# Forty-three offsets to the ranks of a list scheduler, in a fused cosine-attention and highway kernel

## The chip, the cores and the metric

The kernel runs on one core of a Trainium2 chip. The metric is the device time of one execution in microseconds (us). A core has TensorE (PE: matmuls; PEld is its weight load), VectorE (DVE), ScalarE (ACT), GpSimd (POOL) and SyncE (SP, which here only issues DMAs). Each engine executes its own instructions in the order in which the program lists them, and waits on semaphores for what others produce.

## The reference

Eight batches of twelve heads, 448 positions of 64 elements; the result goes as 3584 tokens of 768 into a highway layer.

```python
def _attn_ref(q, k, v, tau):                       # q, k, v: (8, 12, 448, 64)
    q_n = q / (np.linalg.norm(q, axis=-1, keepdims=True) + 1e-06)
    k_n = k / (np.linalg.norm(k, axis=-1, keepdims=True) + 1e-06)
    scores = np.matmul(q_n, k_n.transpose(0, 1, 3, 2)) / tau
    attn = softmax(scores)                          # rows
    return np.matmul(attn, v)

def _moe_ref(x, w_h, w_t, b_t):                     # x: (3584, 768), w: (768, 768)
    H = np.maximum(x @ w_h, 0.0)
    T = 1.0 / (1.0 + np.exp(-(x @ w_t + b_t)))
    return T * H + (1.0 - T) * x

x = _attn_ref(q, k, v, tau).transpose(0, 2, 1, 3).reshape(3584, 768)
out = _moe_ref(x, w_h, w_t, b_t)
```

## The kernel before

**The attention part** goes through 24 *quads* of four heads of one batch (three quads to a batch). A quad's steps, with the line at which the profile shows them:

- *load*: `load_qk` loads q and k as f32 (L312, issued by SP), `load_v` loads v (L334). Six buffers hold raw q and k, two hold v.
- *squares* (L395 on ScalarE, L397 on VectorE, L399 and L411 on GpSimd: two halves), for some quads *folds* on GpSimd that add halves of the squares (L459, L465), and sums of each head on VectorE (L432).
- *inverse root*: for the first quads on ScalarE by a logarithm and an exponential (L488, L497); later, for a batch at a time, on VectorE, by a shift (L521), a subtraction from a constant (L527) and two Newton steps of three operations (L547, L549, L551).
- *norms* (L588, GpSimd or VectorE): raw times inverse root, in f16 as `qn`; then `qn` is transposed to `qT`, on TensorE (L616) with a copy (L622 and 623), or by a DMA that SP issues (L636).
- *scores*: `quad` has seven column groups; for each TensorE multiplies into the tile `sp` (L692, 4 products, or 8 for a pair of groups), and ScalarE takes the exponential of it with 1/tau into `e` (L703). No maximum is subtracted, since cosines are bounded.
- *probabilities times V* in two rounds: `av` (L743), six groups of 14 products, then two groups, into one PSUM tile `u` (a single buffer). The column of V beyond the 64 holds a constant, so that the row sum comes out too. VectorE takes the reciprocal (L776) and scales into the f16 tile `x` (L794; L786 for the tail rows of two batches).
- *cast of v* to f16 as `vm` (L655, VectorE or ScalarE).

**The feed-forward part** takes the 28 tiles of 128 tokens as soon as their x is complete. x is transposed to `xT` (L842 on TensorE, or L851 as a DMA from SP). Then `quarters` runs four passes: halves 0 and 1 of 384 columns, w_t first and w_h second in each half. A pass is two groups of three matmuls (L886, 128x128 by 128x384), in one PSUM tile. It lands in `pt` or, for w_t in the last six tiles, in `sp`; both names have two buffers. The bias is added by a matmul with a row of ones or on VectorE (L904). ScalarE takes the tanh of the w_t pass (L914). The weights are loaded by GpSimd's queue in four halves (L356; the third and fourth are w_h).

The sigmoid is written by tanh; its factor of two is in the V column. For most tiles VectorE ends a half with `fd` (L972: relu of H minus x), `fh` (L957: times 1+tanh) and `fr` (L979: plus 2x). Some tiles have a gate instead: GpSimd computes (tanh−1)·x in two steps (L925, L929) or VectorE in one (L918), and VectorE ends with `fh` (L957) and `fo` (L964: relu, minus the gate). SP stores the result (L1003, L1009).

**What sets the order.** All steps are recorded as operations of a `Plan` with an engine, an estimated duration, a due time (`pri`) and the operations they need; an operation's number is the order in which it was recorded. Buffers enter as needs (`buf`): the n-th user of a ring of tiles needs all users of the tile that it overwrites. `run` first works out due times backwards from the users of each operation. Then it is a list scheduler: it keeps a clock for each engine in its own model of the chip, and takes the ready operation with the smallest key, in which the due time enters with a weight:

```python
k = (max(s, t + self.NEAR) + (e != "SP") * self.LATE * 1000 * o.pri
     + (e == "PE" and o.kind != mode) * self.MODE, o.pri, o.n)
```

Operations marked "lock" are VectorE operations that the model does not let run beside a GpSimd operation. The order found is the order in which the instructions are emitted. Nothing of the model is in the program: on the chip only the order on each engine and the semaphores count. Between the due times and the scheduler stand these lines, which with an empty `NUDGE` do nothing:

```python
for n, shift in self.NUDGE.items():
    self.ops[n].pri += shift
```

Of the kernel before, what the change touches and what calls it, by code (L numbers as in the profile page):

```python
# [20 lines left out]
class Plan:  # L21
# [9 lines left out]
    LATE = 0.04  # L31
    MODE = 60
    QUEUE = 3000
    NUDGE = {}

    def __init__(self):
        self.ops = []
# [20 lines left out]
    def run(self):  # L58
# [31 lines left out]

        for n, shift in self.NUDGE.items():
            self.ops[n].pri += shift
# [1003 lines left out]
```

## Time and profile before

| | before |
|---|---|
| median of 9 runs | 267.87 us (266.84 to 272.14) |
| the profiled execution | 267.87 us |
| its span, first to last instruction | 266.10 us |
| around the span | 1.77 us |
| mean granted TensorE clock | 0.976 |
| DMA | 58.39 MB, mean 219 GB/s |
| scores L692 | 672 products, 53.5 us |
| exponentials L703 | 168 of 128x896, 926 ns each, 145.6 us |
| probabilities times V L743 | 2688 products, 53.9 us |
| feed-forward matmuls L886 into pt and sp | 672, 114.3 and 13.7 us |

A row of a timeline gives the start and the length in us, the engine, the line, the operation, the output from the input, its shape and how many stand in the row; in brackets the idle time of that engine before it and what was seen to end it. Matmuls overlap: the row of three feed-forward matmuls has 0.65 us, but three rows in a line follow each other at 0.49.

### The profile page before, as it was taken

How to read it: one execution, taken by the hardware profiler on the slowest of the kernel's cores; microseconds unless marked ns; L12 is line 12 of the kernel's file. 1: busy time of each engine (PE TensorE's matmuls, PEld its weight loads, DVE VectorE, ACT ScalarE, POOL GpSimd, SP SyncE). 2: the span in 40 equal slices, each digit the busy share in tenths (PEclk: the TensorE clock that was granted, in tenths of full speed). 3: DMA queues.
4: the chain of work that ended last, by engine and by line, in shares of the span. 5: the costliest groups of instructions: out<-in, count | busy, mean ns of one | idle time of the engine just before them, and what ended most of it. 6: DMA issues, size and time to landing. Idle time of an engine off the chain costs nothing.

```text
span 266.1 us, 9994 instructions
## 1 busy us (share of the span) xinstructions
PE 238.6 (90%) x4252; PEld 137.0 (51%) x4252; DVE 223.1 (84%) x493; ACT 213.3 (80%) x295; POOL 148.7 (56%) x164
## 2 busy tenths in 40 slices
PE   7378666989889999999999999999999999997991
PEld 2135453655546655555555555455555655564650
DVE  3988866899999899898998899989998476479983
ACT  4699999699998999999788978989897888820220
POOL 1289586945584975799649941898163004550000
PEclk9858999999999999999999999999999999999998
DMA  6999999988998999999999999999997951216413
GB/s 204 343 381 367 266 266 247 267 257 263 284 330 271 226 245 268 275 169 199 272 342 167 287 251 212 277 195 200 152 262 118 148 130 39 79 42 156 142 60 118
DMA packets 69853, 58.39 MB, mean 219 GB/s; under 512 B 46128, under 2 KB 66096, under 8 KB 69808
## 3 DMA queue, kind: packets, MB, share of 16 engines
q1 hardware_dynamic: 68208, 55.39, 81.5%
q0 software_dynamic: 1600, 2.36, 4.9%
q8 instruction: 33, 0.54, 0.9%
q14 instruction: 12, 0.10, 0.1%
HBM read 38.14 MB, written 11.01 MB: 185 GB/s over the span
## 4 chain that ended last, share of the span: by engine, by line
PE 56%; DVE 18%; ACT 10%; DMA 10%; issue 3%; SPq 1%; POOL 1%; DVEq 0%; ACTq 0%; POOLq 0%
PE pt L886 28%; PE u L743 13%; PE sp L692 11%; ACT e L703 7%; DMA w<-in_moe_w_h_dram 6%; DVE pt L957 3%; DMA raw<-in_q_dram 3%; DVE pt L972 3%; DVE o L979 3%; PE sp L886 2%; DVE x L794 2%; DVE n L432 2%; PE xp L842 2%; ACT sq L395 1%; DMA xT<-x 1%
## 5 line engine op out<-in xcount | busy, mean ns | idle before, releaser
L703 ACT ACTIVATE e<-sp 128x896 f16<-128x896 f32 x168 | 145.6, 926 | 11.2 <-PE sp L692 10.7
L886 PE MATMUL pt<-w,xT 128*128 128x384 f16 x600 | 114.3, 327 | 4.7 <-DMA w<-in_moe_w_h_dram 2.1
L588 POOL TENSOR_TENSOR qn<-raw,rs 128x448 f16<-128x448 f32 x76 | 74.5, 1012 | 38.3 <-DVE rs L551 19.4
L886 PEld LDWEIGHTS <-xT 128*128 128x128 f16 x672 | 60.2, 98 | 54.9 <-issue 17.9
L692 PE MATMUL sp<-qT,qT 64*64 64x448 f16 x672 | 53.5, 373 | 9.0 <-ACT e L703 7.6
L743 PEld LDWEIGHTS <-e 64*128 64x128 f16 x2688 | 46.4, 95 | 19.1 <-issue 13.3
L743 PE MATMUL u<-vm,e 64*128 64x65 f16 x2688 | 53.9, 192 | 0.0
L957 DVE SCALAR_TENSOR_TENSOR pt<-tt,pt 128x384 f32<-128x384 f16 x56 | 31.4, 561 | 6.8 <-PE pt L886 2.5
L459 POOL TENSOR_TENSOR fold<-sq 128x448 f32<-128x448 f16 x24 | 24.7, 1039 | 14.6 <-ACT sq L395 13.2
L432 DVE TENSOR_REDUCE n<-sq 128x7 f32<-128x448 f16 x48 | 27.7, 608 | 4.9 <-ACT sq L405 3.3
L692 PEld LDWEIGHTS <-qT 64*64 64x64 f16 x672 | 15.1, 105 | 32.1 <-issue 27.8
L972 DVE SCALAR_TENSOR_TENSOR pt<-pt,x 128x384 f32<-128x384 f32 x40 | 22.5, 563 | 8.5 <-PE pt L886 7.1
L914 ACT ACTIVATE tt<-pt 128x384 f16<-128x384 f32 x44 | 22.0, 499 | 8.9 <-PE pt L886 4.0
L395 ACT ACTIVATE sq<-raw 128x896 f16<-128x896 f32 x29 | 27.8, 966 | 0.2 <-DMA raw<-in_q_dram 0.2
L794 DVE TENSOR_TENSOR x<-u,rd 128x384 f16<-128x384 f32 x48 | 24.6, 551 | 0.6
L979 DVE SCALAR_TENSOR_TENSOR o<-x,pt 128x384 f32<-128x384 f16 x40 | 22.1, 552 | 1.0
L914 ACT ACTIVATE tt<-sp 128x384 f16<-128x384 f32 x12 | 5.9, 491 | 20.7 <-DVE sp L904 18.9
L399 POOL TENSOR_TENSOR sq<-raw 128x448 f16<-128x448 f32 x14 | 13.1, 937 | 10.2 <-DMA raw<-in_k_dram 10.2
L886 PE MATMUL sp<-w,xT 128*128 128x384 f16 x72 | 13.7, 326 | 1.7 <-DMA xT<-x 1.7
L776 DVE RECIPROCAL rd<-u 128x12 f32<-128x12 f32 (+1 forms) x48 | 9.7, 201 | 5.4 <-PE u L743 5.0
L411 POOL TENSOR_TENSOR sq<-raw 128x448 f16<-128x448 f32 x14 | 13.2, 940 | 0.0
L655 DVE CAST vm<-vr 128x448 f16<-128x448 f32 (+1 forms) x21 | 12.6, 621 | 0.1
(59 smaller groups left out, 188.4 us busy)
## 6 DMA issues: line engine op xcount, KB each, us to landing
vr<-in_v_dram SPq DMA_DIRECT2D x24, 448.0 KB, 7.1
raw<-in_q_dram SPq DMA_DIRECT2D x23, 448.0 KB, 5.5
raw<-in_k_dram SPq DMA_DIRECT2D x23, 448.0 KB, 6.1
out_dram<-o SPq DMA_DIRECT2D x24, 384.0 KB, 4.1
out_dram<-o SPq DMA_DIRECT2D x8, 192.0 KB, 2.7
w<-in_moe_w_t_dram POOLq DMA_DIRECT2D x2, 576.0 KB, 12.1
w<-in_moe_w_h_dram POOLq DMA_DIRECT2D x2, 576.0 KB, 15.7
qT<-qn SPq DMA_TRANSPOSE x34, 3.8
```

The costliest lines, as they stand in the source:

```text
L395: nc.scalar.activation(o, i, AF.Square)
L432: nc.vector.reduce_sum(n2[:, qd, NT * t + g0 : NT * t + g0 + n], src()[:, g0 : g0 + n, 0:width], axis=AX.X,)
L588: (nc.vector if eng == "DVE" else nc.gpsimd).tensor_mul(st["qn", Q, t][:, :, :].rearrange("p c (h d) -> p h c d", h=2)[:, h0:h1, c0:c1, :] ...
L692: nc.tensor.matmul(sp[64 * half : 64 * half + 64, h, 0:S].rearrange("x (c p) -> x c p", c=C), lhsT=kT[hp, ci, 64 * half : 64 * half + 64], ...
L703: nc.scalar.activation(e[:, o : o + 2 * S].rearrange("x (a p c) -> x a p c", a=2, c=C), st["sp", Q, ci][:, :, 0:S].rearrange("x a (c p) -> ...
L743: nc.tensor.matmul(u[:, s, slot * (D + 1) : (slot + 1) * (D + 1)], lhsT=e[sp, o : o + 128], rhs=vm[sp, 2 * qd + h, c, 0 : D + 1], start=(c ...
L794: nc.vector.tensor_mul(st["x", b][:, :, 4 * qd : 4 * qd + 4, :].rearrange("p t (h s) d -> p t h s d", s=2)[:, :, :, s, :], u[:, s, :, 0:D] ...
L886: nc.tensor.matmul(loc["pt", qi], lhsT=loc["xT"][:, cc, :] if cc < CC else ones_row[:, :], rhs=w_f[w_i][:, cc, ms] if cc < CC else bth[:, ms],
L914: nc.scalar.activation(loc["tt", mh][:, :], loc["pt", qi], AF.Tanh)
L957: nc.vector.scalar_tensor_tensor(out=h, in0=loc["tt", mh][:, :], scalar=1.0, in1=h, op0=ALU.add, op1=ALU.mult)
L972: nc.vector.scalar_tensor_tensor(out=h, in0=h, scalar=0.0, in1=xf()[:, ms], op0=ALU.max, op1=ALU.subtract)
L979: nc.vector.scalar_tensor_tensor(out=loc["o"][:, ms], in0=xf()[:, ms], scalar=2.0, in1=loc["pt", qi], op0=ALU.mult, op1=ALU.add,)
```

## The change

`NUDGE` gets 43 entries: number of an operation, and the shift of its due time in us (negative: earlier). Nothing else is changed; the instructions are the same ones. Since the due time enters the key with weight 0.04, a shift of 10 us is worth 0.4 us of start time in the model, and one early choice can move later ones.

```diff
-    NUDGE = {}
+    NUDGE = {
+        63: -57.5, 121: -57.5, 147: -1, 172: 5, 264: -57.5, 314: 12, 407: 3.5, 427: 12.5, 441:
+        -2.5, 445: 3.5, 454: 1.5, 455: -46, 459: -1, 491: 8, 527: 4, 532: 3.5, 693: 65.5, 707:
+        4, 736: -16.5, 747: 4, 790: 4, 828: 15.5, 871: 10, 976: 8.5, 1001: 3, 1024: -10.5, 1055:
+        2.5, 1068: -7, 1240: 29.5, 1316: 0.5, 1340: 2, 1346: 16, 1366: -8.5, 1369: -24, 1426:
+        37, 1466: -2.5, 1467: -16.5, 1468: -4.5, 1560: 8.5, 1568: 15, 1576: 2, 1581: 15, 1588:
+        58,
+    }
```

By engine, the smallest number of operations whose moving turns the one order into the other: TensorE 29 of 571 (a group of matmuls is one operation), VectorE 63 of 488, ScalarE 16 of 295, GpSimd 12 of 159, SP 12 of 157. TensorE's order differs around 24 to 41 us of the profile of before, 58 to 63, 200, 208 and 227 to 242; from 63 to 198 us its operations stand in the same order. ScalarE's differs around 27 to 64 and 144 to 151.

The moves of which the prediction speaks, with the place in time that the operation had in the profile of before:

| operations | what they are | how they move |
|---|---|---|
| 121 | VectorE, sum of squares of quad 3, half of k | ahead of other steps, near 24 us |
| 445, 172, 491 | ScalarE: a cast of v, squares of quad 8, an exponential of quad 4 | behind their neighbours, 46 to 64 us |
| 790 and neighbours | VectorE, a feed-forward end step near 97 us | behind a reciprocal (operation 671) |
| 693, 976, 1024 | GpSimd, norms of quads 8, 13 and 14 | among GpSimd's other steps |
| 264, 265, 266 | VectorE, inverse root of the fifth batch (L521, L527, L547) | 265 and 266 behind three end steps and a cast, 129 to 134 us |
| 276 | VectorE, squares (L397, 142.78 us) | ahead of the L972 at 139.04 us |
| 314 | GpSimd, squares (L411, 178.95 us) | behind the gate step L925 (183.54), ahead of its L929 (184.53) |
| 1466–1468, 1472, 1473 | TensorE, probabilities times V of quad 22 | some groups earlier among the feed-forward matmuls, from 227 us |
| 1560, 1568, 1576, 1581 | TensorE, groups of three feed-forward matmuls | 1568 and 1581 behind the probabilities times V of the last quad (237.64) |
| 1569, 1570 | VectorE, `fh` L957 (236.34) and `fo` L964 (239.22) | behind the scaling of the last quad (L794, 239.95) |

## Prediction

> **What bounds the kernel now.** The page came first: the busy shares and the chain that ended last.
>
> ```profile
> PE 238.6 (90%) x4252; PEld 137.0 (51%) x4252; DVE 223.1 (84%) x493; ACT 213.3 (80%) x295; POOL 148.7 (56%) x164
> PE 56%; DVE 18%; ACT 10%; DMA 10%; issue 3%; SPq 1%; POOL 1%; DVEq 0%; ACTq 0%; POOLq 0%
> ```
>
> TensorE is 90% busy and holds over half of the chain. The change adds and removes no instruction, so it can only shorten or lengthen waits, and where TensorE loses time decides. The table of windows of 10 us says where (columns: PE, PEld, DVE, ACT, POOL busy, clock, DMA share, GB/s):
>
> ```profile
> 30.00:40.00 10.00, 6.04 (x170) 4.43 (x167) 7.32 (x14) 10.00 (x15) 9.16 (x10) 1.00 1.11 264
> 40.00:50.00 10.00, 7.58 (x162) 4.55 (x158) 6.88 (x14) 8.21 (x13) 7.73 (x9) 1.00 0.98 234
> 130.00:140.00 10.00, 9.22 (x184) 5.00 (x185) 9.56 (x24) 7.84 (x11) 4.18 (x5) 1.00 1.04 286
> 180.00:190.00 10.00, 9.52 (x175) 5.27 (x176) 9.76 (x24) 8.93 (x12) 5.29 (x6) 1.00 0.85 190
> 240.00:250.00 10.00, 8.35 (x77) 5.00 (x76) 9.39 (x20) 1.47 (x3) 0.00 (x0) 1.00 0.62 156
> ```
>
> Before 80 us TensorE is short of work while ScalarE is full (10.00 in 30–40). From 80 to 240 us TensorE is busy at 9.2 to 10.0, and a delay of it is carried on, since no slack is left to absorb it; a saving likewise. From 240 us VectorE (9.39) is the fuller engine: it runs eight steps of 0.56 us at a pitch of 0.47 to 0.66 for each tile of the feed-forward stage, while TensorE needs 4 × 0.98 = 3.9 us.
>
> Next the timelines around each place where the order differs.
>
> ```profile
> 46.44 0.65 PE L886 MATMUL pt<-w,xT 128*128 128x384 f16 x3 [2.05 <-DMA w<-in_moe_w_h_dram]
> 132.73 1.14 PE L886 MATMUL pt<-w,xT 128*128 128x384 f16 x6 [0.34 <-DVE o L979]
> 189.94 0.65 PE L886 MATMUL pt<-w,xT 128*128 128x384 f16 x3 [0.42 <-DVE o L979]
> 243.90 1.15 PE L886 MATMUL sp<-w,xT 128*128 128x384 f16 x6 [1.66 <-DMA xT<-x]
> ```
>
> These four stalls of TensorE, 4.5 us together, are what a new order could reach.
>
> **Part 1, up to 64 us (thirteen shifts): nothing, −0.3 to +0.3.** At 46.44 the queue of TensorE stands until the last half of w_h has landed, and the chain shows 14.79 us of that transfer. Its issue (L356, GpSimd, 31.61 us) waits behind two normalisations on GpSimd. In the new order the sum of squares that they depend on is taken earlier, and the issue would come at about 29.8. But the weight queue q0 carries 2.36 MB from 25 to 46 us without a gap, sharing the engines with the loads of q1: it is never dry, so an earlier issue of the last piece lands at the same time. The changed steps of TensorE, ScalarE and VectorE ahead of the barrier are the same set in both orders and all reach it, since TensorE has 2.05 and ScalarE (next row, 47.46) 0.89 us to spare. On SP a load of q for quad 9 passes a transposition (issue 45.49); the transpositions have 5 us or more from landing to first use. Behind the barrier three ScalarE steps swap places (exponentials, one squaring, one cast); counted through, ScalarE comes to the same step at 64.3 instead of 64.2.
>
> **Part 2, 64 to 128 us: +0.1 (0 to +0.2).** Near 97 us a reciprocal of 0.2 us moves ahead of L957 and its L979, whose reader on TensorE had 0.07 us to spare: 0.2 − 0.07 ≈ 0.1. Other moves (GpSimd's norms for quads 13 and 14, L979 and L957 at 113) have covers of 1 us and more.
>
> **Part 3, 128 to 146 us: −0.5 (−0.9 to +0.4).** Now the first steps of an inverse root stand in the middle of VectorE's evictions:
>
> ```profile
> 129.59 1.08 DVE L527 TENSOR_SCALAR rs<-rs 128x84 int32<-128x84 int32 x1
> 187.65 0.20 DVE L527 TENSOR_SCALAR rs<-rs 128x84 int32<-128x84 int32 x1
> 129.57 1.03 POOL L459 TENSOR_TENSOR fold<-sq 128x448 f32<-128x448 f16 x1
> 136.43 8.22 POOL L588 TENSOR_TENSOR qn<-raw,rs 128x448 f16<-128x448 f32 x8 [5.82 <-DVE rs L551]
> 142.78 1.07 DVE L397 TENSOR_TENSOR sq<-raw 128x896 f16<-128x896 f32 x1
> ```
>
> The same step takes 1.08 us beside a GpSimd fold that ends with it, and 0.20 alone: 0.88 is waiting for GpSimd. The change puts L521 and L527 behind three evictions and a cast, so these come up to 1.3 us sooner and the 0.34 stall at 132.73, plus 0.1 to 0.2 of its after-effect, goes: −0.5. Against it, the squaring L397 (now 142.78) moves ahead of the L972 at 139.04, that is, into GpSimd's run of eight norms of 1.03 each. If it waits as L527 did, it costs up to 0.9 there, and the stall saved comes back: +0.4. I take −0.5, because L397 at 142.78 also lies in that run (136.43 to 144.65) and took 1.07, hardly more than its work. The Trainium skill ("SBUF — State Buffer", Terms) says that the two engines share a port pair that is held for a whole instruction and blocks the other fully. By that rule alone the moved L397 could wait for a whole norm, and this part would be +0.4 instead of −0.5; it speaks against this move.
>
> **Part 4, 176 to 192 us: +0.5 (+0.2 to +1.1).** On GpSimd the second half of a squaring (L411) moves from ahead of one gate to between two gate steps:
>
> ```profile
> 178.95 0.95 POOL L411 TENSOR_TENSOR sq<-raw 128x448 f16<-128x448 f32 x1
> 183.54 0.91 POOL L925 TENSOR_TENSOR g<-tt,x 128x384 f16<-128x384 f16 x1
> 184.53 0.92 POOL L929 TENSOR_TENSOR g<-g,x 128x384 f16<-128x384 f16 x1
> 185.95 0.56 DVE L964 SCALAR_TENSOR_TENSOR o<-pt,g 128x384 f32<-128x384 f32 x1
> ```
>
> L925 waits for ScalarE's gate and so starts no earlier than 183.5; L411 then runs from 184.5, and L929 ends at 186.35 instead of 185.45. VectorE's L964 starts at about 186.4 instead of 185.95, and TensorE, which reuses its bank, had 0.17 to spare: +0.28. VectorE's later evictions start by as much later, two small steps come ahead of them, and the reader at 189.94, already late by 0.42, pays about 0.2 more: +0.5. The lower end is the first term less a little; the upper end charges all of L411's 0.95 and 0.15 of the small steps. TensorE is 9.97 to 10.0 busy behind it, so this is carried to the tail. On SP a load of v passes from 180.5 to about 190 and its reader, a ScalarE cast at 197.65, keeps the 7.1 us that such a load takes, just covered.
>
> **Part 5, the tail from 226 us: −1.0 (−1.5 to +0.2).** Four rows show it:
>
> ```profile
> 237.64 1.50 PE L743 MATMUL u<-vm,e 64*128 64x65 f16 x84
> 239.22 0.56 DVE L964 SCALAR_TENSOR_TENSOR o<-pt,g 128x384 f32<-128x384 f32 x1 [0.57 <-POOL g L929]
> 239.95 1.02 DVE L794 TENSOR_TENSOR x<-u,rd 128x384 f16<-128x384 f32 x2
> 245.47 0.56 DVE L904 SCALAR_TENSOR_TENSOR sp<-b_all,sp 128x384 f32<-128x384 f32 x1
> 253.42 0.56 DVE L957 SCALAR_TENSOR_TENSOR pt<-tt,pt 128x384 f32<-128x384 f16 x1 [0.47 <-DVE pt L972]
> ```
>
> The last quad's probabilities·V (84 products, 237.64) now stand behind four groups of three feed-forward matmuls that move behind them. Two of these (0.98 us) and the wait for the earlier u buffer go ahead of it no more, so the products start at about 236.3. VectorE's L964, which stood idle 0.57 us for GpSimd at 239.22, and its L957 (236.34) move behind L794, so L794 ends at about 239.2 instead of 240.97: −1.8. The transposition of x leaves SP as much sooner (241.03 to 239.2), lands 2.8 us later at 242.1 instead of 243.9, and TensorE fills the 1.66 of the wait with the groups moved back. But what ends the kernel is VectorE: it works without a gap from 240.88 to 245.47, the first bias step of the last tiles, and now has the two moved evictions in that stretch, 2 × 0.5 = 1.0. So the bias step comes 1.8 − 1.0 = 0.8 sooner, at 244.7, and TensorE's product for it, done at 243.3, is not late. Then VectorE's run stays as it is, but for the pause of 0.47 at 253.42: its inputs were there 0.4 us before, so no operand held it, and it stands once in 20 us. I count half of it as gone: −0.2. Ends: without the idle stretches at 234 to 239 (0.57, 0.15, 0.41, 0.35) VectorE could save 1.5 us; and if TensorE's groups of which two wait for VectorE's evictions come late, +0.2.
>
> **Sum.** 0 + 0.1 − 0.5 + 0.5 − 1.0 = −0.9. The profiled execution took 267.87 us, span 266.10 and 1.77 around it, and the median of the nine runs is also 267.87. So 267.87 − 0.9 ≈ 267.0. Adding the ends one way gives −2.3 to +1.4, but they do not fall together; half of that either side gives the forecast's own range, 265.9 to 267.8. About 0.3%, 0.8 us, is what a measurement can tell, so faster means below 267.07.
>
> **The rivals.** *The barrier moves, faster:* if more of the software queue's pieces in flight gives it a larger share, w_h lands up to 1.8 us sooner (31.61 − 29.8), and TensorE's 2.05 with it. For it: it is the largest stall in the chain. Against: 576 KB take 15.7 us to land at an even rate. ScalarE, full on both sides, has 0.89 idle there, and this is what it could gain: −0.9 and the forecast's −0.9 are −1.8, or 266.1. With the whole 1.8 gained, and the other half of the pause in the tail, it is 267.9 − 1.8 − 0.9 − 0.2 = 265.0. *The GpSimd place, slower:* L411 between the gate steps. It decides from the point where L929 ends later than about 186.2 (185.45 now, with 0.45 of VectorE's slack and 0.17 of TensorE's): at +1.1, and the stall of part 3 merely moved by L397 (+0.4 for −0.5), the total is 0.1 + 0.4 + 1.1 − 0.8 = +0.8, or 268.7. For it: GpSimd's rows are serial and TensorE is full. *VectorE eats the tail:* the two moved evictions cost 0.7 each, the widest pitch, and the pause stays: tail −1.8 + 1.4 = −0.4; the sum is −0.3, or 267.6. *The order does not bite:* nine of the 43 keep their own place on their engine, 29 of TensorE's 571 groups move, and waits undo the rest: 267.9.
>
> **How the numbers follow.** Forecast 0.50: its range lies above 267.07 by four parts in ten, so 0.32 faster and 0.18 same. Barrier 0.18, all faster. GpSimd 0.18, slower. VectorE 0.09 and no bite 0.05, same, with 0.02 of the first slower. Together faster 0.50, same 0.30, slower 0.20. The low end 265.0 reaches to the barrier's far side, the high end 268.8 to the GpSimd case; outside them no more than 2 in 10 is left.
>
> **What would show it.** Right: the row of 46.44 still with about 2 us of wait on w_h; the 0.34 of 132.73 gone; a wait of 0.7 or more ahead of one product near 190; the wait on the transposition near 242 gone, the last L794 ending some 1.8 us sooner measured from the end of part 4, and VectorE without gaps from there. Wrong: a shorter wait on w_h, a row of L397 above 1.5 us near 139, L929 ending before 186, or a last bias sequence that starts less than 0.4 or more than 1.2 us sooner than the shift of TensorE at 230 us explains.

## The result

The changed kernel takes 266.47 us (median of 16 runs, 264.66 to 267.44) beside 268.21 us before (53 runs). The ratio is 0.9927, 95% interval 0.9906 to 0.9948: 1.4 to 2.5 us faster, 1.96 in the middle. 267.0 was forecast, from a median of 267.87. Against the larger sample of before, the forecast's −0.9 us has the right sign and less than half of the size.

The page of the changed kernel (span 264.6 us; the seven lines of the diff move all later line numbers by 7, so L972 is now L979, and L979 is L986):

```profile
PE 240.7 (91%) x4252; PEld 137.5 (52%) x4252; DVE 223.3 (84%) x493; ACT 213.4 (81%) x295; POOL 150.0 (57%) x164
```

The counts are the old ones. The busy times of VectorE and ScalarE differ by 0.2 us or less, TensorE's is 2.1 and GpSimd's 1.3 us higher. A row's length is therefore not work alone (a GpSimd norm below takes 0.94 or 1.86 us); what raised these two sums as a whole was not traced. The windows that answer to those shown of before:

```profile
130.00:140.00 10.00, 10.00 (x191) 5.40 (x190) 9.02 (x23) 8.34 (x12) 5.91 (x7) 1.00 0.97 260
180.00:190.00 10.00, 9.33 (x169) 5.14 (x167) 9.71 (x25) 8.48 (x12) 4.73 (x6) 1.00 0.68 110
240.00:250.00 10.00, 9.74 (x58) 5.48 (x57) 9.30 (x21) 1.96 (x4) 0.00 (x0) 1.00 0.79 159
```

TensorE gained 0.78 in 130 to 140 and 1.39 in 240 to 250, and lost 0.19 in 180 to 190. Its timeline at the places in question:

```profile
47.46 0.65 PE L893 MATMUL pt<-w,xT 128*128 128x384 f16 x3 [1.50 <-DMA w<-in_moe_w_h_dram]
60.36 0.49 PE L849 MATMUL xp<-ident,x 128*128 128x128 f16 x6 [0.37 <-DVE o L986]
189.66 0.65 PE L893 MATMUL pt<-w,xT 128*128 128x384 f16 x3 [0.62 <-DVE o L986]
236.33 1.50 PE L750 MATMUL u<-vm,e 64*128 64x65 f16 x84
242.07 1.15 PE L893 MATMUL sp<-w,xT 128*128 128x384 f16 x6
247.32 1.14 PE L893 MATMUL pt<-w,xT 128*128 128x384 f16 x6 [0.19 <-DVE o L986]
248.29 1.14 PE L893 MATMUL sp<-w,xT 128*128 128x384 f16 x6
249.38 1.14 PE L893 MATMUL pt<-w,xT 128*128 128x384 f16 x6
```

The wait on w_h stands, the stall of 0.34 at 132.7 is gone, the one at 190 has grown from 0.42 to 0.62, the 1.66 on the last transposition is gone (the row at 242.07 has no bracket). A wait of 0.37 at 60 us is new. In the tail some passes follow each other at 1.09 (248.29 to 249.38) instead of 0.98.

**A way to read the whole trace.** Since all instructions are the same, each TensorE operation can be compared with itself: its start in one profile minus its start in the first profile of before. The shift at one moment is worth little (at 46.4 us the profiles differ by up to 1.2 us); what counts is how it changes from column to column. Columns are places in the first profile of before, in us:

| shift of TensorE, us | 46.4 (after w_h) | 63.1 | 83.5 | 127.7 | 152.4 | 189.9 | 226.2 | 237.6 | 243.9 | 259.2 |
|---|---|---|---|---|---|---|---|---|---|---|
| before, second profile | +0.67 | +0.67 | +0.67 | +0.66 | +0.62 | +0.64 | +0.64 | +0.64 | +0.65 | +0.66 |
| changed | +1.01 | +1.36 | +0.84 | +0.65 | −0.56 | −0.27 | −0.27 | −1.31 | −1.82 | −1.45 |
| changed, second profile | +0.27 | +0.62 | +0.11 | +0.07 | −1.13 | −0.82 | −0.82 | −1.86 | −2.38 | −2.00 |
| only_early | −0.11 | +0.25 | −0.26 | −0.45 | −1.01 | −1.02 | −1.02 | −1.02 | −1.01 | −1.33 |
| only_six_early | +0.15 | +0.15 | −0.49 | −0.47 | −0.92 | −0.93 | −0.93 | −0.93 | −0.92 | −0.93 |
| only_693 | +0.34 | +0.33 | +0.34 | +0.78 | +0.34 | +0.35 | +0.35 | +0.35 | +0.34 | +0.03 |
| only_middle | −0.03 | −0.04 | −0.03 | −0.01 | −1.22 | −1.20 | −1.20 | −1.20 | −1.19 | −1.51 |
| only_gpsimd | +0.40 | +0.40 | +0.41 | +0.42 | −0.02 | +0.27 | +0.27 | +0.28 | +0.28 | +0.28 |
| only_tail | +0.32 | +0.32 | +0.33 | +0.34 | −0.10 | −0.10 | −0.10 | −1.14 | −1.67 | −1.27 |
| only_two_tail | +0.58 | +0.58 | +0.58 | +0.57 | +0.35 | +0.36 | +0.36 | −0.35 | −0.88 | −0.03 |
| after_no_gpsimd | −0.03 | +0.35 | −0.15 | −0.34 | −1.54 | −1.53 | −1.53 | −2.57 | −3.08 | −2.70 |
| after_no_late_bias | +1.12 | +2.01 | +1.51 | +1.40 | +0.20 | +0.50 | +0.50 | −0.54 | −1.05 | −1.36 |
| six_early_rest | +0.57 | +0.57 | −0.06 | −0.01 | −1.21 | −1.20 | −1.20 | −2.24 | −2.75 | −2.01 |

From the product that waited for w_h to the end, the changed kernel is 2.46 us shorter in its first profile and 2.27 in its second. What is won or lost in one stretch stays: from 152 to 226 us the shifts do not move but at the GpSimd place. The kernels other than before and changed are those of the experiments below.

### The profile page after: what moved, and what is told of

Its sections match the earlier page's. It is cut to its first block, busy times and chain, and to the rows that moved or that the text cites. A ratio compares the mean times of both kernels' runs of the same rounds, so it can differ in the third digit from the quotient of the medians.

```text
span 264.6 us, 9988 instructions
## 1 busy us (share of the span) xinstructions
PE 240.7 (91%) x4252; PEld 137.5 (52%) x4252; DVE 223.3 (84%) x493; ACT 213.4 (81%) x295; POOL 150.0 (57%) x164
## 4 chain that ended last, share of the span: by engine, by line
PE 56%; DVE 17%; DMA 11%; ACT 8%; issue 3%; SPq 2%; POOL 1%; DVEq 0%; ACTq 0%
PE pt L893 29%; PE u L750 13%; PE sp L699 11%; ACT e L710 6%; DMA w<-in_moe_w_h_dram 6%; DMA raw<-in_q_dram 3%; DVE pt L964 3%; DVE o L986 2%; DVE pt L979 2%; DMA vr<-in_v_dram 2%; DVE n L439 2%; PE xp L849 2%; DVE x L801 1%; DVE sp L911 1%; SPq L319 1%
## 5 line engine op out<-in xcount | busy, mean ns | idle before, releaser
L750 PEld LDWEIGHTS <-e 64*128 64x128 f16 x2688 | 47.2, 95 | 20.2 <-issue 13.7
L750 PE MATMUL u<-vm,e 64*128 64x65 f16 x2688 | 55.1, 192 | 0.5 <-DVE xtail L793 0.2
L964 DVE SCALAR_TENSOR_TENSOR pt<-tt,pt 128x384 f32<-128x384 f16 x56 | 31.4, 561 | 6.6 <-PE pt L893 2.9
L979 DVE SCALAR_TENSOR_TENSOR pt<-pt,x 128x384 f32<-128x384 f32 x40 | 22.5, 562 | 7.3 <-PE pt L893 4.2
L986 DVE SCALAR_TENSOR_TENSOR o<-x,pt 128x384 f32<-128x384 f16 x40 | 22.1, 552 | 0.9
L406 POOL TENSOR_TENSOR sq<-raw 128x448 f16<-128x448 f32 x14 | 13.2, 947 | 11.4 <-DMA raw<-in_k_dram 11.2
L418 POOL TENSOR_TENSOR sq<-raw 128x448 f16<-128x448 f32 x14 | 13.9, 993 | 0.0
L662 DVE CAST vm<-vr 128x448 f16<-128x448 f32 (+1 forms) x21 | 13.2, 656 | 0.1
```

Source lines behind the costliest of these rows:

```text
L750: nc.tensor.matmul(u[:, s, slot * (D + 1) : (slot + 1) * (D + 1)], lhsT=e[sp, o : o + 128], rhs=vm[sp, 2 * qd + h, c, 0 : D + 1], start=(c ...
L964: nc.vector.scalar_tensor_tensor(out=h, in0=loc["tt", mh][:, :], scalar=1.0, in1=h, op0=ALU.add, op1=ALU.mult)
L979: nc.vector.scalar_tensor_tensor(out=h, in0=h, scalar=0.0, in1=xf()[:, ms], op0=ALU.max, op1=ALU.subtract)
L986: nc.vector.scalar_tensor_tensor(out=loc["o"][:, ms], in0=xf()[:, ms], scalar=2.0, in1=loc["pt", qi], op0=ALU.mult, op1=ALU.add,)
```

## The experiments

Each kernel has a subset of the entries in `NUDGE`, so the change falls into four parts that can be run apart. TensorE's order then differs from the old one only in that part's stretch. One part reaches further on another engine: with the early shifts VectorE's order differs between 133 and 146 us too (casts, sums and the squaring L397 change places). Six to twelve runs stand behind each median.

| kernel | median, us | ratio to before, 95% interval |
|---|---|---|
| only_early | 267.67 | 0.9978 (0.9959 to 0.9996) |
| only_middle | 267.09 | 0.9965 (0.9944 to 0.9986) |
| only_gpsimd | 268.35 | 1.0017 (0.9992 to 1.0042) |
| only_tail | 266.90 | 0.9951 (0.9929 to 0.9973) |
| after_no_gpsimd | 265.71 | 0.9911 (0.9880 to 0.9943) |
| after_no_late_bias | 265.72 | 0.9907 (0.9875 to 0.9938) |
| only_six_early | 266.91 | 0.9965 (0.9943 to 0.9987) |
| only_two_tail | 267.36 | 0.9976 (0.9949 to 1.0004) |
| six_early_rest | 265.96 | 0.9922 (0.9894 to 0.9950) |

The four parts add to 0.9978 + 0.9965 + 1.0017 + 0.9951 − 3 = 0.9911, beside 0.9927 (0.9906 to 0.9948) for all together: they are additive within what the runs can tell, which is some 0.004 for the sum of four.

**The early part.**

```diff
-    NUDGE = {}
+    NUDGE = {121: -57.5, 147: -1, 172: 5, 407: 3.5, 427: 12.5, 441: -2.5, 445: 3.5,
+             454: 1.5, 455: -46, 459: -1, 491: 8, 527: 4, 532: 3.5, 693: 65.5}
```

> Only the fourteen shifts whose operations stand before 80 us. Theory (the wait on w_h at 46.4 us stands where it stood, and all that is moved ahead of it reaches it): 0, that is within 0.3% of before, and TensorE's wait on w_h about 2 us. Rival (the early order passes the barrier): 0.9 to 1.8 us faster, the wait on w_h shorter by as much.

It is faster, by 0.1 to 1.1 us. The interval takes in the theory's "within 0.3%" as well as the lower end of the rival; the traces speak against both: w_h did not land sooner, and TensorE does win something behind the barrier. The product that waits for w_h starts at 46.33 instead of 46.44, with 1.67 us of wait in the place of 2.05: TensorE came later to a barrier that stood still. How long it waits there says when it arrived, and not when w_h landed: in its second profile the changed kernel waits only 0.47 us, and its product yet starts 0.27 us later than that of before. Counted from the issue of the first weight load, the last half of w_h lands after 25.04 and 25.07 us in the two profiles of before, and after 24.87 to 25.15 us in the five with the full early order. Its issue, however, came only 0.4 to 0.6 us sooner there (9.69 to 9.88 us after the first, instead of 10.25), and not the 1.8 that the prediction had counted on: what so early an issue would do was not tried.

```profile
46.71 0.65 PE L893 MATMUL pt<-w,xT 128*128 128x384 f16 x3 [0.47 <-DMA w<-in_moe_w_h_dram]
```

Behind the barrier the early order first loses (−0.11 to +0.25 at 63 us; the changed kernel +0.35 in both profiles, with TensorE's new wait on L986 at 60 us; after_no_late_bias, in the same order, +0.89) and then wins 0.50 to 0.52 by 83.5 us. So the question was which of its moves win there.

```diff
-    NUDGE = {}
+    NUDGE = {445: 3.5, 172: 5, 491: 8, 532: 3.5, 527: 4, 693: 65.5}
```

> Only the shifts 445, 172, 491, 532, 527 and 693: TensorE's order and all that stands ahead of 53 us are as before; ScalarE, VectorE and GpSimd change places between 53 and 78 us. Theory (what the early shifts bring is won behind the barrier, where sums of VectorE move out of the way of an L979 at 78.6 us): 0.2 to 0.6 us faster, TensorE's waits on L979 at 74 and 79 us (0.37 and 0.46) smaller. Rival (it is won ahead of the barrier): within 0.2 of before.

The first theory holds: TensorE's shift falls by 0.64 from 46.4 to 83.5 us (+0.15 to −0.49), none of it ahead of 63 us, and these six have no loss at 60 us. What went are two waits that the old timeline has and the prediction had not looked at (the new rows, at 73.83 and 78.87 us, have no wait):

```profile
74.11 1.14 PE L886 MATMUL pt<-w,xT 128*128 128x384 f16 x6 [0.37 <-DVE o L979]
79.36 0.49 PE L842 MATMUL xp<-ident,x 128*128 128x128 f16 x6 [0.46 <-DVE o L979]
```

VectorE's timeline, before, shows two sums (L432) in a row ahead of the L979 that TensorE waits for at 79.36:

```profile
78.17 0.67 DVE L432 TENSOR_REDUCE n<-fold 128x14 f32<-128x224 f32 x2
78.77 0.54 DVE L979 SCALAR_TENSOR_TENSOR o<-x,pt 128x384 f32<-128x384 f16 x1
```

With the six shifts the first sum stands ahead of L964, where VectorE had 0.1 us of idle time, and the L979 (now L986) starts 0.49 sooner:

```profile
77.23 0.38 DVE L439 TENSOR_REDUCE n<-fold 128x14 f32<-128x224 f32 x1
78.28 0.55 DVE L986 SCALAR_TENSOR_TENSOR o<-x,pt 128x384 f32<-128x384 f16 x1
```

The sum could start there because GpSimd's folds come 0.6 us sooner (74.07 instead of 74.64). Of this only GpSimd's order was tried alone:

```diff
-    NUDGE = {}
+    NUDGE = {693: 65.5}
```

> Only the shift 693: one of GpSimd's norms of quad 8 behind its neighbours at 73 to 78 us; all other engines in the order of before. Theory (it takes VectorE's earlier sum and a GpSimd fold that comes sooner together): TensorE's wait of 0.46 on L979 at 79.36 stands. Rival (GpSimd's order alone does it): that wait is gone.

```profile
79.70 0.49 PE L849 MATMUL xp<-ident,x 128*128 128x128 f16 x6 [0.46 <-DVE o L986]
```

The wait stands at 0.46, and TensorE's shift does not move from 46 to 84 us. But alone, this shift does not bring the folds forward either: they start at 74.97 instead of 74.64, as much later as all the rest. So the gain needs some of the other five shifts, which move ScalarE's and VectorE's steps; which of them was not tried.

**The middle part**, eighteen shifts:

```diff
-    NUDGE = {}
+    NUDGE = {63: -57.5, 264: -57.5, 707: 4, 736: -16.5, 747: 4, 790: 4, 828: 15.5, 871: 10,
+             976: 8.5, 1001: 3, 1024: -10.5, 1055: 2.5, 1068: -7,
+             1316: 0.5, 1340: 2, 1346: 16, 1366: -8.5, 1369: -24}
```

> Only the eighteen shifts from 84 to 209 us, without the two of GpSimd near 180 us. Theory (the stall of 0.34 at 132.73 goes with the inverse-root steps out of the way): 0.4 to 0.7 us faster, all of it won between 130 and 141 us. Rival (the squaring L397, moved into GpSimd's run of norms, waits for the shared port and gives it back): 0 to 0.4 us slower, with a row of L397 above 1.5 us near 139.

It is faster by 0.4 to 1.5 us. The shift falls by 1.21 between 127.7 and 152.4 us, and by 1.20 or 1.21 in every other kernel with this order: 0.50 or 0.51 at 132.7 us and the rest near 140. The rival fails. VectorE's rows in the changed kernel:

```profile
131.81 0.20 DVE L534 TENSOR_SCALAR rs<-rs 128x84 int32<-128x84 int32 x1
137.94 1.08 DVE L404 TENSOR_TENSOR sq<-raw 128x896 f16<-128x896 f32 x1
```

The subtraction takes 0.20 instead of 1.08, with GpSimd idle beside it, and the squaring takes 1.08 inside GpSimd's run of eight norms (135.26 to 143.77), no more than where it stood. It was GpSimd that waited there. The norm beside the squaring takes 1.86, another of the same run 0.94; in the old order, too, the norm beside the squaring of 142.78 takes 1.96:

```profile
136.16 0.94 POOL L595 TENSOR_TENSOR qn<-raw,rs 128x448 f16<-128x448 f32 x1
137.95 1.86 POOL L595 TENSOR_TENSOR qn<-raw,rs 128x448 f16<-128x448 f32 x1
142.69 1.96 POOL L588 TENSOR_TENSOR qn<-raw,rs 128x448 f16<-128x448 f32 x1
```

Of the 1.21, some 0.76 is the order's. Four kernels that leave this stretch as it was (only_six_early, only_693, only_gpsimd, only_tail) also win 0.44 or 0.45 there, because the first profile of before has a wait of TensorE of 0.67 at 140.23 us that none of the other 13 profiles has: they gain 0.73 by that product and give back 0.28 or 0.29 by 142 us. The kernels with the new order do not give that back, which with the 0.50 at 132.7 makes the 0.76. The second profile of before lacks that wait, yet loses 0.42 at 132.7 instead: VectorE's shift takes 0.62 beside a GpSimd squaring (0.22 in the first), which had itself waited 0.37 for a load:

```profile
130.00 0.62 DVE L521 TENSOR_SCALAR rs<-n 128x84 int32<-128x84 int32 x1
129.62 0.93 POOL L411 TENSOR_TENSOR sq<-raw 128x448 f16<-128x448 f32 x1
```

only_two_tail has a weaker form of this (0.45), and wins 0.22; only_early wins 0.56 with VectorE's other order.

**The GpSimd part.**

```diff
-    NUDGE = {}
+    NUDGE = {314: 12, 1240: 29.5}
```

> Only the two shifts 314 and 1240: the half of a squaring L411 behind the gate step L925. Theory: 0.3 to 0.5 us slower, L929 ending at about 186.3, TensorE losing the time between 184 and 191 us. Rival (VectorE's other order there takes it back): 0, no stall of TensorE above the 0.42 that stood there.

```profile
185.07 0.92 POOL L936 TENSOR_TENSOR g<-g,x 128x384 f16<-128x384 f16 x1
190.21 0.65 PE L893 MATMUL pt<-w,xT 128*128 128x384 f16 x3 [0.62 <-DVE o L986]
```

The runs alone are unclear (1.0017, with 1 inside the interval). The trace is clear: the second gate step ends at 185.99 instead of 185.45 with TensorE at the same time (shift −0.02) ahead of it, and TensorE loses 0.29 between 152 and 190 us and keeps that to the end. The changed kernel loses 0.29 and, in its second profile, 0.31 at the same place. Taken out of the change:

```diff
-        -57.5, 314: 12, 407: 3.5, ... 1068: -7, 1240: 29.5, 1316: 0.5, ...
+        -57.5, 407: 3.5, ... 1068: -7, 1316: 0.5, ...
```

> The changed kernel without its two shifts 314 and 1240, so with GpSimd's half squaring where it stood. Theory (that move alone costs 0.29 in the trace and is carried to the end): 0.3 us faster than the changed kernel, that is a ratio of 0.991 to 0.992 to before, and the wait on L979's eviction near 190 us at 0.42 instead of 0.62. Rival (it helps something later): as the changed kernel or slower, 0.993 or above.

0.9911 is where the theory put it, though the interval takes in the rival as well; the trace has no loss at 190 us (−1.54 to −1.53). With 265.71 us (six runs) it has the lowest median of all versions with the full computation; its interval overlaps that of the changed kernel.

**The tail**, nine shifts:

```diff
-    NUDGE = {}
+    NUDGE = {1426: 37, 1466: -2.5, 1467: -16.5, 1468: -4.5,
+             1560: 8.5, 1568: 15, 1576: 2, 1581: 15, 1588: 58}
```

> Only the nine shifts of the tail (1426 and from 1466 on). Theory (the last transposition of x starts 1.8 us sooner and VectorE gives 1.0 of it back): 0.8 to 1.3 us faster, TensorE's wait on the transposition gone, VectorE's last L794 ending 1.3 to 1.8 us sooner. Rival (VectorE eats the gain): 0.4 us faster at most, with VectorE's last operations as late as before.

Faster by 0.7 to 1.9 us. The trace wins 1.04 by the last probabilities times V (237.6), 1.57 by the pass behind the transposition, gives back 0.40 and keeps 1.17. The changed kernel has 1.18 in both profiles, after_no_gpsimd 1.17. All four profiles lack VectorE's pause of 0.47 near 253 us; with it, in six_early_rest, the same order keeps 0.81. Two shifts alone:

```diff
-    NUDGE = {}
+    NUDGE = {1568: 15, 1581: 15}
```

> Only the shifts 1568 and 1581: two groups of feed-forward matmuls behind the last probabilities times V, the other probabilities times V where they stood. Theory (these two carry the tail's gain): 1.0 to 1.4 us faster, as the nine shifts of the tail. Rival (the earlier products of quad 22 are needed for it): 0.6 us or less.

The rival is nearer: 0.6 us in the runs (−0.1 to 1.4, which takes in both), 0.39 in the trace. These two bring 1.24 of the 1.57 up to the transposition, but then 0.85 is lost by 259 us, where VectorE, which has next to no idle time from 239 us on, holds TensorE's banks. The other seven shifts, three of which bring products of quad 22 forward, are worth the rest; they were not run one by one.

What bounds the tail was tried by taking VectorE's work away:

```diff
-                if not by_mm:
+                if not by_mm and n < 24:
```

> The changed kernel, but VectorE's bias step L904 is left out for the last three tiles that have one (six steps of 0.56 us, 2.8 to 3.3 us of VectorE's work at the end; the gate of these tiles then lacks the bias). Theory of the prediction (VectorE's work ends the kernel): 2 us or more faster than the changed kernel, about 264.3. Rival (TensorE's sixteen passes of 0.98 us from the last transposition on end it, and VectorE only holds a bank now and then): at most 0.6 us faster, about 265.9, TensorE's rows then 0.98 apart without a gap.

```profile
242.85 1.15 PE L893 MATMUL sp<-w,xT 128*128 128x384 f16 x6
248.71 1.14 PE L893 MATMUL sp<-w,xT 128*128 128x384 f16 x6
249.69 1.14 PE L893 MATMUL pt<-w,xT 128*128 128x384 f16 x6
257.81 1.14 PE L893 MATMUL pt<-w,xT 128*128 128x384 f16 x6
```

TensorE's passes now stand 0.98 apart throughout, but for two bias products of 0.16: the first to the last takes 257.81 − 242.85 = 14.96 us, beside 257.73 − 242.07 = 15.66 with the bias. So 2.8 us less of VectorE's work brought 0.70 to TensorE, and 264.5 − 242.85 = 21.65 instead of 264.6 − 242.07 = 22.53 to the end: 0.9. The time of 264.3 (a ratio of 0.9865 to the 267.92 that before took beside these runs) lies outside the interval. TensorE's passes set the end, and VectorE adds some 0.7 to them.

**Combined and repeated.**

```diff
-    NUDGE = {}
+    NUDGE = {445: 3.5, 172: 5, 491: 8, 532: 3.5, 527: 4, 693: 65.5,
+             ... the eighteen of the middle, the nine of the tail
+    }
```

> The six early shifts 445, 172, 491, 532, 527 and 693, and all later shifts but 314 and 1240: the changed kernel without its eight other early shifts, and without the GpSimd move. Theory (each part is carried to the end and they add up: −0.6 for the six, −0.75 for the middle, −1.2 for the tail): 2.5 to 2.9 us faster than before, a ratio of 0.989 to 0.991, slightly below the 0.9911 of the changed kernel without the GpSimd move. Rival (the other early shifts are worth having, 0.3 us by the wait of 0.41 on VectorE at 90 us that goes with them): 0.992 or above.

0.9922: a miss on the ratio. By the table it did avoid the loss at 60 us (+0.57 to +0.57), but it did not get the 0.27 or 0.28 that kernels with the full early order gain near 93 us (and of which they give back 0.08 to 0.23 by 100 us), where VectorE otherwise waits 0.40 to 0.41 ahead of an L972. That wait stands in both profiles of before and in the seven kernels without the eight other early shifts, and in none of the five profiles with them. And it lost 0.74 between 243.9 and 259.2, where after_no_gpsimd lost 0.38: it has the pause near 253 us. With these intervals the runs do not rank the two.

> The changed kernel, unchanged, for a second profile. Theory: from TensorE's product after the wait on w_h to the end it is 2.0 us shorter than before, as in its first profile, whatever the time at which w_h lands. Rival (part of that was of the one execution): less than 1.5 us.

2.27 us, with a landing of w_h that was 0.75 sooner: the gain is of the order and not of one execution.

> The kernel before, unchanged, for a second profile. Theory (TensorE's 0.67 at 140.23 us and VectorE's pause of 0.47 at 253.42, which no operand explains, belong to that one execution): the first is gone, as in the parts that do not touch that place; the 0.34 at 132.7 and the 1.66 at 243.9 stand. Rival (they belong to the order): both stand.

Two rows of it, TensorE's and VectorE's:

```profile
133.81 1.14 PE L886 MATMUL pt<-w,xT 128*128 128x384 f16 x6 [0.76 <-DVE o L979]
254.07 0.56 DVE L957 SCALAR_TENSOR_TENSOR pt<-tt,pt 128x384 f32<-128x384 f16 x1 [0.47 <-DVE pt L972]
```

Half right. The 0.67 at 140.23 is gone, but 0.42 more is lost at 132.7, by the longer shift shown above, so the stretch takes as long as in the first profile. The pause of 0.47 is there again.

## Why the prediction was right or wrong

- *Part 1, the barrier at 46 us: right, on a lighter test than meant.* The landing of w_h did not move with the early order, but its issue came 0.4 to 0.6 us sooner and not 1.8. TensorE's wait on w_h became shorter, which was named as a sign of being wrong; TensorE came later, and w_h no sooner. *The steps to 64 us: wrong in size.* They were said to be 0; the changed kernel loses 0.35 by 63 us, with a new wait of 0.37 on an L979 of VectorE, ahead of which a step of the inverse root (L521, 0.2) now stands. ScalarE's steps alone had been counted through. In after_no_late_bias the loss is 0.89; there that step takes 0.64 instead of 0.18, and TensorE waits 0.87 for an exponential.
- *Part 2, 64 to 128 us: wrong in sign.* +0.1 was put down, from one move near 97 us. That move cost 0.02 (only_middle, 83.5 to 127.7 us). What was missed is the gain at 74 and 79 us, 0.5 to 0.6, from VectorE's sums and inverse-root steps, and the wait at 92 us. Net of the loss at 60 us, the early order is worth 0.20 to 0.36 by 127.7 us in four profiles, costs 0.28 in that of after_no_late_bias, and is worth 0.1 to 1.1 in the runs.
- *Part 3: right mechanism, too small.* −0.5 was the stall at 132.73 and its after-effect; it measured 0.50 at that place. Some 0.26 more near 140 us was not foreseen. The bound of +0.4 did not come in, and the reason given (the squaring takes hardly more than its work among norms of 1.03 each) misread a mean: seven of the eight norms take 0.94, and the one beside the squaring 1.96. The rule of the Trainium skill ("SBUF — State Buffer", Terms), by which the shared port pair is held for a whole instruction and the loser blocks fully, fits both rows: GpSimd's fold held up VectorE's subtraction (1.08 for 0.20), and VectorE's squaring held up GpSimd's norm (1.86 for 0.94). The prediction had the rule, but asked only whether VectorE would wait.
- *Part 4: right mechanism, +0.5 for a measured 0.29.* The first term was 0.28, in part by chance, since L964 started 0.32 later and not 0.45. The 0.2 on top of it did not come: L411 stood in the way of the gate step L925, which now starts 0.2 sooner, so the second gate step ends 0.56 later and not 0.9.
- *Part 5: right mechanism, −1.0 for a measured 1.17.* Each step was too large: 1.04 for 1.3 at the products, 1.57 for 1.8 at the transposition, and 0.4 instead of 0.8 given back. "What ends the kernel is VectorE" was the step that failed: the sixteen passes of 0.98 us end it, and VectorE adds what it holds up of them. The pause of 0.47, counted by half, is in no settled relation to the change: it stands in both profiles of before, in only_gpsimd, only_six_early and six_early_rest, and in none of the other nine. Profiles without it lose 0.3 to 0.4 us less at the end, so that much of the 1.17 is not shown to be the order's.
- *The sum.* Early −0.3, middle −0.8, GpSimd +0.3, tail −1.2 make −2.0, beside −1.96 (−1.4 to −2.5) in the runs. The forecast of 267.0 and its range hold the time of 266.47, but parts 1 and 2 together, 3, 4 and 5 were all off to the same side, and the gain is twice the one forecast. The ends of the five parts add up to −2.5 and +2.2, and not to −2.3 and +1.4 as the prediction has it, so its range was drawn too narrow by its own rule.
- *The rivals.* The barrier did not move; the GpSimd place cost a quarter of the price that its rival put on it. VectorE did not eat the tail: it kept 1.17 and not 0.4. And the order does bite.

## What to carry to other kernels

When a change only reorders, compare each operation of the bounding engine with itself and read where the shift changes: a gain of 0.5 us that a time cannot show is then plain, and so is a loss that should be taken out. List all waits of the bounding engine in every stretch that the new order touches, also the small ones: here two waits of 0.4 on an eviction were worth more than the 2 us at a barrier that stands on a transfer. Two engines that are both nearly full in a tail were told apart here by taking work from one of them. And where two engines can hold each other up, look at the rows of both: here the longer row was the other engine's.

## What the hardware did that was not expected

- VectorE and GpSimd hold each other up by as much as a whole instruction, in either direction. VectorE's subtraction of 128x84 took 1.08 us beside one GpSimd fold and 0.20 without; VectorE's squaring of 128x896 took 1.08 us (137.94 in the changed kernel) inside a run of GpSimd norms, and the norm beside it took 1.86 instead of 0.94. A mean over the eight norms (1.03) hides this.
- VectorE has pauses of 0.41 and 0.47 us that no operand explains, at the same instructions in several kernels and not in others whose neighbouring instructions are the same. They are worth some 0.3 us each, and what decides on them stays open.
- The first profile of before has a wait of TensorE of 0.67 us at 140.23 that no other of the 14 profiles has and for which nothing in the trace is seen to be the cause. Until more profiles were read, it made the gain of the middle part look 0.44 us larger. So two profiles alone tell a change to about half a microsecond.
